# Four units with u kept as pairs of tokens and transposed as 32-bit words, with two decays on VectorE and two output copies on ScalarE

## The chip, the cores and the metric

The kernel runs on one core of a Trainium2 chip. The core has a matrix engine (TensorE, PE in the profile, with its weight loads as PEld), VectorE (DVE), ScalarE (ACT), GpSimd (POOL) and SyncE (SP), which here only issues DMAs. The metric is the device time of one execution in microseconds (us); of several runs the median is given.

## What is computed

A gated recurrence over tokens, followed by a highway layer. The inputs are x and f_logit (4 sequences of 6336 tokens, 256 channels, float32), a lower bound for each channel, two 256 x 256 weights and a bias.

```python
sig = 1.0 / (1.0 + np.exp(-f_logit))
f = lower_bound + (1.0 - lower_bound) * sig
i = 1.0 - f
for t in range(S):                       # each of the 4 sequences on its own
    h = f[:, t] * h + i[:, t] * x[:, t]
    y[:, t] = h
H = np.maximum(y @ w_h, 0.0)
T = 1.0 / (1.0 + np.exp(-(y @ w_t + b_t)))
out = T * H + (1.0 - T) * y
```

## The kernel before

The 25344 tokens are cut into 21 units. A unit has one sub-unit or, in the middle of the kernel (units 7 to 13), two; a full sub-unit is 1024 tokens. A sub-unit is loaded with tokens across the 128 partitions, eight tokens to a partition, so a tile of x or of f_logit is 128 x 8 x 256. The scan needs the other layout, channels across partitions and tokens along them, and the 256 channels make two halves. So TensorE transposes on the way in, and the product with an identity brings the result back on the way out.

All work is written out by hand in one string, `order`. Each token of it is one step, and each engine carries out its steps in that order. A token is a letter, the unit, and then sub-unit and half (or chunk and half); the number behind the colon is a buffer or, for steps that write PSUM, the banks; a `v` at the end puts a step on VectorE that stands elsewhere without it. The letters:

- `l`, `x`: loads of f_logit and x (SyncE issues them). `w`: the store of a block of output.
- `u` (L273, ScalarE): u = sigmoid(-f_logit), written as 16-bit floats. `f8.1` means unit 8, half 1; `u8.1` unit 8, sub-unit 1.
- `i` (L297, TensorE): transposes u into PSUM, one 128 x 128 block for each of eight tokens. `f` (L312 on ScalarE, L310 on VectorE): the decay, f = 1 - (1 - lower_bound) u, read from these banks and written to SBUF with the tokens in order. The transposed blocks lie token by token (j, then p), and f wants p, then j, so f reads with a hop at every element.
- `b`, `B` (L288, GpSimd): the product of u and x, half a sub-unit or a whole one. It is stored in pairs of tokens, so that `p` (L322, TensorE) can transpose two 16-bit tokens as one 32-bit word, four transposes for a half in place of eight.
- `s` (L331, VectorE): the scan along the tokens, over the decays and over the transposed products in PSUM, in pieces where a sequence begins inside a unit. It carries the state from unit to unit.
- `z`, `g` (L344 and L149, TensorE): the two products with the weights. `t` (L367, ScalarE): the sigmoid of z. `d` (L374, VectorE): the larger of g and a multiple of y. `e`, `E` (L388, GpSimd, or VectorE with `v`): d times t.
- `o` (L407 and L408, TensorE): back to tokens across partitions, summed in PSUM. `c` (L427 on ScalarE, L425 on VectorE): the copy of that to SBUF, from which the store goes.

PSUM has eight banks, and the string says which bank each step uses. A step that writes a bank waits until the step that read it before is done. Four such places matter later. In unit 8 the transposes i8.1.1 and i8.0.1 fill banks 6 and 7, f8.1 reads them, and g6.0.0 writes the same two. The outputs o4.0.0 and o4.0.1 share banks 2 and 3, with the copy c4.0.0 between them. The sigmoid t11.1.0 reads banks 6 and 7 before z12.1.0 writes them. The product g12.0.0 feeds d12.0.0 and needs the scan s12.1 before it.

The order of these steps around the first place stands in the string so:

```python
o4.0.0:23 p7.1.1:67 z6.0.1:45 x8.0:4 u8.1:2 c4.0.0v:2 t6.0.1:0 d6.0.1:2 p7.0.1 o4.0.1:23 c4.0.1:1 s7.1:2 i7.0.0:01
x8.1:0 i7.1.0 f7.0:2 p7.1.0:45 w3.0.1 w3.0.0 i8.0.0:23 i8.1.0 l9.0:1 p7.0.0 s7.0:3 l9.1:2 E5.0 f8.0:0 z6.0.0:01 t6.0.0
i8.1.1:67 i8.0.1 f8.1:1 o5.0.0:23 o5.0.1:01 B8.0:0 b8.1.1:1 g6.0.0:67 b8.1.0 d6.0.0 E6.0 g7.1.1:45 d7.1.1:3 w4.0.1
```

Of the kernel before, what the change touches and what calls it, by code (L numbers as in the profile page):

```python
# [91 lines left out]
w11.0.1 u17.0:3 z13.0.1:45 x20.0:3 d13.1.1:2 g13.0.1:23 d13.0.1 B15.0:0 w11.1.0 l20.0:0 w11.1.1 g13.1.0:01 t13.0.1:1
u16.0:1 o12.1.0:67 d13.1.0 p14.0.1:4 s14.1:4 c12.1.0:3 x16.0:0 z13.1.0:23 t13.1.0:2 o12.0.1:01 p14.0.0:5 z13.0.0:67
z13.1.1:23 c12.0.1:2 t13.0.0 s14.0:5 t13.1.1 o12.1.1:01 c12.1.1:1 i17.0.1:4 e13.0.1 o12.0.0:67 i17.0.0:2 p15.0.1:3
# [175 lines left out]
    def do_u(eng, slot, n, s):  # L270
        nb = units[n][1][s]
        u = sb([P, NB, D], FP16, "u", slot)
        pin(nc.scalar.activation(u[:, :nb], st[n]["l", s][:, :nb], AF.Sigmoid, scale=-1.0))  # L273
# [8 lines left out]
    def products(eng, slot, n, s, k0, k1):
        if ("bv", s) not in st[n]:
            st[n]["bv", s] = sb([P, NB // 2, D, 2], BF16, "bv", slot)
        cuts = {2: (0, 1), 4: (0, 1, 2), 8: (0, 2, 4)}[units[n][1][s]]
# [2 lines left out]
        shared(pin(e.tensor_mul(st[n]["bv", s][:, a:c].rearrange("p k d j -> p k j d"),  # L288
                                st[n]["u", s][:, 2 * a:2 * c].rearrange("p (k j) d -> p k j d", j=2),
                                st[n]["x", s][:, 2 * a:2 * c].rearrange("p (k j) d -> p k j d", j=2))), not eng)  # L290

    def do_i(eng, slot, n, s, h):
        if ("uT", h) not in st[n]:
            st[n]["uT", h] = Banks(slot, FP16)
        uT = st[n]["uT", h].one(s)
        for j in range(units[n][1][s]):
            pin(nc.tensor.transpose(uT[:, j * P:(j + 1) * P], st[n]["u", s][:, j, h * P:(h + 1) * P], ident_h))  # L297

    def do_f(eng, slot, n, h):
        N, subs = tokens(n), units[n][1]  # L300
        f = sb([P, 2 * NB * P], FP16, "f", slot)
        to, of = f[:, :N], st[n]["uT", h].all(N)
        if len(subs) == 1:
            to = to.rearrange("c (p j) -> c p j", j=subs[0])
            of = of.rearrange("c (j p) -> c p j", j=subs[0])
        else:
            to = to.rearrange("c (s p j) -> c s p j", s=len(subs), j=subs[0])
            of = of.rearrange("c (s j p) -> c s p j", s=len(subs), j=subs[0])
        if eng:
            pin(nc.vector.tensor_scalar(to, of, ncc[:, h:h + 1], 1.0, op0=ALU.mult, op1=ALU.add))  # L310
        else:
            pin(nc.scalar.activation(to, of, AF.Identity, scale=ncc[:, h:h + 1], bias=1.0))  # L312
        st[n]["f", h] = f

    def do_p(eng, slot, n, s, h):
        if ("bT", h) not in st[n]:
# [1 line left out]
        words = st[n]["bT", h].one(s).bitcast(FP32)
        g = units[n][1][s] // 2
        for k in range(g):  # L320
            pair = st[n]["bv", s][:, k, h * P:(h + 1) * P].rearrange("p d j -> p (d j)").bitcast(FP32)
            pin(nc.tensor.transpose(words[:, k:k + g * (P - 1) + 1:g], pair, ident_f))  # L322
# [152 lines left out]
```

## Time and profile before

| | us |
|---|---|
| median of 3 runs | 207.34 (206.93 to 207.41) |
| span of the profiled execution (first to last instruction) | 205.8 |
| busy: PE / DVE / ACT / POOL | 194.8 / 192.4 / 190.7 / 173.8 |
| scans (L331), 40 of one form group | 103.7 |
| products of u and x on GpSimd (L288), 39 | 101.4 |
| gates on GpSimd (L388), 33 | 71.5 |
| decays on ScalarE (L312), 38 | 50.3 |
| u on ScalarE (L273), 28 | 48.1 |
| output copies on ScalarE (L427), 46 | 44.2 |

Of the profiled execution the views give its span; what lies around the span shows in the difference to the runs. A row of a group names line, engine, operation, what is written and read with its shape, how often, the busy time, the mean time of one in ns, and the idle time before with what ended it. A row of a timeline has start, length, engine, line and operation; equal neighbours are merged with their count. TensorE's matmuls overlap, so a row's length there is longer than its share of the engine's time. The granted clock of TensorE is 0.998 over the span.

### The profile page before, as it was taken

The page shows a single profiled execution, that of the slowest core. Times are in us where ns is not written, and L with a number is a line of the kernel's source. Part 1 is how long each engine was busy: PE and PEld are TensorE (multiplying, and loading weights), DVE is VectorE, ACT ScalarE, POOL GpSimd, SP SyncE. Part 2 cuts the span into 40 slices and gives each one's busy share as a digit, 9 for nine tenths or more (in the row PEclk, how much of TensorE's full clock was granted, in tenths as well). Part 3 has the DMA queues.
Part 4 walks back from the last instruction along what each step waited for, and adds up shares of the span by engine and source line. Part 5 has one row for each costly group of instructions (what it writes and reads, how often), then busy time and mean ns, then how long its engine had stood idle before and what let it go on. Part 6 is the DMA issues. An engine that isn't in the chain of part 4 may idle for free.

```text
span 205.8 us, 4646 instructions
## 1 busy us (share of the span) xinstructions
PE 194.8 (95%) x1850; PEld 135.7 (66%) x1850; DVE 192.4 (93%) x147; ACT 190.7 (93%) x182; POOL 173.8 (84%) x85
## 2 busy tenths in 40 slices
PE   7989999969989999999999999999999999999992
PEld 2555775746765747757757858657757868777671
DVE  0679999999999999999999999999999999999992
ACT  5197999999999999999999999999999999999992
POOL 3634696999999999979999869999899788999760
PEclk9999999999999999999999999999999999999999
DMA  6999999999999999999999999999999999853766
GB/s 191 375 427 419 417 420 419 414 413 426 416 426 427 414 422 410 432 408 427 426 408 426 427 412 425 419 422 427 414 411 407 334 411 382 344 212 140 277 225 234
DMA packets 16700, 78.67 MB, mean 382 GB/s; under 512 B 1828, under 2 KB 2344, under 8 KB 10792
## 3 DMA queue, kind: packets, MB, share of 16 engines
q1 hardware_dynamic: 16672, 78.39, 93.9%
q8 instruction: 14, 0.23, 0.4%
q14 instruction: 6, 0.05, 0.1%
q10 hardware_dynamic: 8, 0.00, 0.0%
HBM read 52.43 MB, written 25.95 MB: 381 GB/s over the span
## 4 chain that ended last, share of the span: by engine, by line
PE 56%; DVE 24%; ACT 7%; issue 5%; DMA 5%; SPq 0%; DVEq 0%; ACTq 0%
PE psum L344 17%; DVE y L331 15%; PE psum L149 13%; DVE d L374 7%; PE psum L407 7%; PE psum L408 7%; PE psum L322 6%; PE psum L297 5%; ACT f L312 4%; DMA x<-in_x_dram 4%; ACT t L367 2%; DMA l<-in_f_logit_dram 1%; ACT u L273 1%; PE psum L250 1%; ACT o L427 1%
## 5 line engine op out<-in xcount | busy, mean ns | idle before, releaser
L288 POOL TENSOR_TENSOR bv<-u,x 128x1024 bf16<-128x1024 f16 (+2 forms) x39 | 101.4, 2615 | 20.0 <-DVE d L388 10.9
L331 DVE TENSOR_TENSOR_SCAN y<-f,y,psum 128x1024 bf16<-128x1024 f16 (+6 forms) x40 | 103.7, 2612 | 0.5 <-PE psum L407 0.4
L344 PE MATMUL psum<-y,w_sb 128*128 128x512 bf16 (+1 forms) x240 | 79.6, 368 | 4.2 <-ACT f L312 1.9
L388 POOL TENSOR_TENSOR d<-d,t 128x1024 bf16<-128x1024 bf16 (+3 forms) x33 | 71.5, 2180 | 4.6 <-ACT o L427 1.3
L374 DVE SCALAR_TENSOR_TENSOR d<-y,ncc,psum 128x1024 bf16<-128x1024 bf16 (+2 forms) x60 | 62.7, 1084 | 1.1 <-PE psum L344 0.4
L149 PE MATMUL psum<-y,w_sb 128*128 128x512 bf16 x168 | 63.6, 379 | 0.0
L367 ACT ACTIVATE t<-psum,bt 128x1024 bf16<-128x1024 f32 (+2 forms) x60 | 57.4, 988 | 0.9 <-PE psum L344 0.5
L273 ACT ACTIVATE u<-l 128x2048 f16<-128x2048 f32 (+2 forms) x28 | 48.1, 1744 | 6.5 <-DMA l<-in_f_logit_dram 6.5
L312 ACT ACTIVATE f<-psum,ncc 128x1024 f16<-128x1024 f16 (+3 forms) x38 | 50.3, 1344 | 1.2 <-PE psum L297 1.2
L407 PE MATMUL psum<-diag,y 128*128 128x128 f16 x396 | 49.7, 219 | 0.2
L408 PE MATMUL psum<-ident_b,d 128*128 128x128 bf16 x396 | 49.7, 219 | 0.0
L408 PEld LDWEIGHTS <-d 128*128 128x128 bf16 x396 | 43.5, 112 | 3.8 <-DVE d L388 0.4
L427 ACT COPY o<-psum 128x1024 f32<-128x1024 f32 (+1 forms) x46 | 44.2, 997 | 1.6 <-ACT f L312 0.6
L407 PEld LDWEIGHTS <-y 128*128 128x128 bf16 x396 | 43.6, 112 | 2.7
L344 PEld LDWEIGHTS <-w_sb 128*128 128x128 f16 x240 | 23.0, 98 | 20.1 <-issue 0.8
L322 PE MATMUL psum<-ident_f,bv 128*128 128x128 f32 x198 | 29.4, 275 | 0.8 <-ACT f L312 0.7
L149 PEld LDWEIGHTS <-w_sb 128*128 128x128 f16 x168 | 16.4, 97 | 20.2 <-issue 5.9
L297 PE MATMUL psum<-ident_h,u 128*128 128x128 f16 x396 | 28.8, 221 | 0.8 <-DVE y L331 0.4
L297 PEld LDWEIGHTS <-u 128*128 128x128 f16 x396 | 25.1, 99 | 5.7 <-issue 1.2
L322 PEld LDWEIGHTS psum<-ident_f,bv 128*128 128x128 f32 x198 | 22.4, 141 | 5.8 <-ACT f L312 1.4
L388 DVE TENSOR_TENSOR d<-d,t 128x1024 bf16<-128x1024 bf16 (+3 forms) x20 | 11.3, 596 | 0.1
L149 PE MATMUL psum<-zeros 128*128 128x512 bf16 x39 | 10.6, 398 | 0.0
(34 smaller groups left out, 43.1 us busy)
## 6 DMA issues: line engine op xcount, KB each, us to landing
l<-in_f_logit_dram SPq DMA_DIRECT2D x23, 1024.0 KB, 13.6
x<-in_x_dram SPq DMA_DIRECT2D x23, 1024.0 KB, 14.2
out_dram<-o SPq DMA_DIRECT2D x43, 512.0 KB, 8.0
out_dram<-x SPq DMA_DIRECT2D x7, 256.0 KB, 2.0
out_dram<-o SPq DMA_DIRECT2D x6, 256.0 KB, 9.3
l<-in_f_logit_dram SPq DMA_DIRECT2D x2, 512.0 KB, 6.5
x<-in_x_dram SPq DMA_DIRECT2D x2, 512.0 KB, 7.3
l<-in_f_logit_dram SPq DMA_DIRECT2D x3, 256.0 KB, 2.8
```

The lines of the kernel that those rows point to most:

```text
L149: return pe.add_instruction(mybir.InstMatmult(name=nc.get_next_instruction_name(), start_tensor_calc=start, stop_tensor_calc=stop, tile_si ...
L288: shared(pin(e.tensor_mul(st[n]["bv", s][:, a:c].rearrange("p k d j -> p k j d"), st[n]["u", s][:, 2 * a:2 * c].rearrange("p (k j) d -> p ...
L297: pin(nc.tensor.transpose(uT[:, j * P:(j + 1) * P], st[n]["u", s][:, j, h * P:(h + 1) * P], ident_h))
L312: pin(nc.scalar.activation(to, of, AF.Identity, scale=ncc[:, h:h + 1], bias=1.0))
L322: pin(nc.tensor.transpose(words[:, k:k + g * (P - 1) + 1:g], pair, ident_f))
L331: pin(nc.vector.tensor_tensor_scan(y[:, c:e], st[n]["f", h][:, c:e], data, 0.0 if fresh else carry[h], op0=ALU.mult, op1=ALU.add))
L344: pin(nc.tensor.matmul(p.part(a, e), w, data, start=ki == 0, stop=ki == NH - 1))
L367: pin(nc.scalar.activation(half(n, q, "t", m), z, AF.Sigmoid, bias=bt[:, m:m + 1]))
L374: pin(nc.vector.scalar_tensor_tensor(half(n, q, "d", m), y, ncc[:, m:m + 1], g, op0=ALU.mult, op1=ALU.max))
L388: shared(pin(e.tensor_mul(d, d, t)), not eng)
L407: pin(nc.tensor.matmul(o, st[n]["y", h][:, whole], diag[:, h], start=True, stop=False))
L408: pin(nc.tensor.matmul(o, half(n, q, "d", h)[:, cols], ident_b, start=False, stop=True))
```

## The change

In units 8, 10, 14 and 15 u is stored as pairs: for each pair of tokens and each channel the two tokens lie side by side. In units 8 and 14 ScalarE reads f_logit in its own order and writes every second element; in units 10 and 15 it writes in order and reads the two tokens of a pair in turn, 1 KB apart. In all four, TensorE transposes u as it does the products, two tokens in a 32-bit word, and the words land in PSUM so that the tokens are in order. The decay of such a unit then reads and writes in order. The product of u and x reads u and writes in order and reads x at two tokens in turn, 1 KB apart.

Four steps change engines: f8.1 and f14.0 go from ScalarE to VectorE, c4.0.0 and c9.1.1 from VectorE to ScalarE. The string is otherwise the same.

```diff
+    PAIRS_WRITTEN, PAIRS_READ = (8, 14), (10, 15)
+    PAIRS = PAIRS_WRITTEN + PAIRS_READ
...
-o4.0.0:23 p7.1.1:67 z6.0.1:45 x8.0:4 u8.1:2 c4.0.0v:2 t6.0.1:0 d6.0.1:2 p7.0.1 o4.0.1:23 c4.0.1:1 s7.1:2 i7.0.0:01
+o4.0.0:23 p7.1.1:67 z6.0.1:45 x8.0:4 u8.1:2 c4.0.0:2 t6.0.1:0 d6.0.1:2 p7.0.1 o4.0.1:23 c4.0.1:1 s7.1:2 i7.0.0:01
...
         u = sb([P, NB, D], FP16, "u", slot)
-        pin(nc.scalar.activation(u[:, :nb], st[n]["l", s][:, :nb], AF.Sigmoid, scale=-1.0))
+        to, of = u[:, :nb], st[n]["l", s][:, :nb]
+        if n in PAIRS:
+            u = u.rearrange("p j d -> p (j d)").rearrange("p (k d j) -> p k d j", d=D, j=2)
+            of = of.rearrange("p (k j) d -> p k j d", j=2)
+            to = u[:, :nb // 2]
+            if n in PAIRS_WRITTEN:
+                to = to.rearrange("p k d j -> p k j d")
+            else:
+                of = of.rearrange("p k j d -> p k d j")
+        pin(nc.scalar.activation(to, of, AF.Sigmoid, scale=-1.0))
...
+        if n in PAIRS:
+            shared(pin(e.tensor_mul(st[n]["bv", s][:, a:c], st[n]["u", s][:, a:c],
+                                    st[n]["x", s][:, 2 * a:2 * c].rearrange("p (k j) d -> p k d j", j=2))), not eng)
+            return
...
+    def paired(out, of, s, h, g):
+        words = out.one(s).bitcast(FP32)
+        for k in range(g):
+            pair = of[:, k, h * P:(h + 1) * P].rearrange("p d j -> p (d j)").bitcast(FP32)
+            pin(nc.tensor.transpose(words[:, k:k + g * (P - 1) + 1:g], pair, ident_f))
...
+        if n in PAIRS:
+            paired(st[n]["uT", h], st[n]["u", s], s, h, units[n][1][s] // 2)
+            return
...
         to, of = f[:, :N], st[n]["uT", h].all(N)
-        if len(subs) == 1:
+        if n in PAIRS:
+            pass
+        elif len(subs) == 1:
```

**At 50 to 65 us.** On VectorE, from the two steps d5.0.0 and d5.0.1 (first row) to the scans of unit 8. The COPY is c4.0.0, the four scans are s7.1 and s7.0, two pieces each, and the three d behind them are d6.0.0, d7.1.1 and d7.0.1. Before:

```order
35 L374 SCALAR_TENSOR_TENSOR d<-y,ncc,psum 128x1024 x2
36 L425 COPY o<-psum 128x1024
37 L374 SCALAR_TENSOR_TENSOR d<-y,ncc,psum 128x1024
38 L331 SCALAR_TENSOR_TENSOR y<-f,y,psum 128x1216
39 L331 SCALAR_TENSOR_TENSOR y<-f,psum 128x832
40 L331 SCALAR_TENSOR_TENSOR y<-f,y,psum 128x1216
41 L331 SCALAR_TENSOR_TENSOR y<-f,psum 128x832
42 L374 SCALAR_TENSOR_TENSOR d<-y,ncc,psum 128x1024 x3
43 L331 SCALAR_TENSOR_TENSOR y<-f,y,psum 128x2048 x2
```

The same stretch of VectorE with the change, where the first row takes in d6.0.1 as well and f<-psum is f8.1:

```order
35 L396 SCALAR_TENSOR_TENSOR d<-y,ncc,psum 128x1024 x3
36 L353 SCALAR_TENSOR_TENSOR y<-f,y,psum 128x1216
37 L353 SCALAR_TENSOR_TENSOR y<-f,psum 128x832
38 L353 SCALAR_TENSOR_TENSOR y<-f,y,psum 128x1216
39 L353 SCALAR_TENSOR_TENSOR y<-f,psum 128x832
40 L336 TENSOR_SCALAR f<-psum,ncc 128x2048
41 L396 SCALAR_TENSOR_TENSOR d<-y,ncc,psum 128x1024 x3
42 L353 SCALAR_TENSOR_TENSOR y<-f,y,psum 128x2048 x2
```

The copy has left the place ahead of d6.0.1, and f8.1 has come in between the scans of s7.0 and d6.0.0.

On TensorE, at the end of o5.0.1 and the beginning of g6.0.0, with the engines that a row waits for in brackets. Before:

```order
855 L408 MATMUL psum<-ident_b,d 128x128
856 L344 LDWEIGHTS w_sb
857 L344 MATMUL psum<-y,w_sb 128x512 [waits Activation_49]
858 L149 LDWEIGHTS w_sb
859 L149 MATMUL psum<-y,w_sb 128x512
```

And with the change:

```order
795 L430 MATMUL psum<-ident_b,d 128x128
796 L366 LDWEIGHTS w_sb
797 L366 MATMUL psum<-y,w_sb 128x512 [waits DVE_49]
798 L151 LDWEIGHTS w_sb
799 L151 MATMUL psum<-y,w_sb 128x512
```

The order on TensorE is the same, but the first matmul of g6.0.0 now waits for VectorE where it waited for ScalarE.

**At 131 to 138 us.** On ScalarE, from t11.0.0 and t11.1.1 (first row) to the copy c11.0.1; the first COPY is c9.1.0, the two u are u15.0 and u14.0, the t between them is t11.1.0. Before:

```order
82 L367 ACTIVATE t<-psum,bt 128x1024 x2
83 L427 COPY o<-psum 128x1024
84 L273 ACTIVATE u<-l 128x2048
85 L367 ACTIVATE t<-psum,bt 128x1024
86 L273 ACTIVATE u<-l 128x2048
87 L367 ACTIVATE t<-psum,bt 128x1024
88 L427 COPY o<-psum 128x1024
```

With the change:

```order
82 L389 ACTIVATE t<-psum,bt 128x1024 x2
83 L449 COPY o<-psum 128x1024 x2
84 L284 ACTIVATE u<-l 128x2048
85 L389 ACTIVATE t<-psum,bt 128x1024
86 L284 ACTIVATE u<-l 128x4x2x256
87 L389 ACTIVATE t<-psum,bt 128x1024
88 L449 COPY o<-psum 128x1024
```

The copy c9.1.1 has come in ahead of c9.1.0, so u15.0 and t11.1.0 stand one step later; u14.0 is now written in pairs.

More of the change, by code (lines that the diff above doesn't have):

```diff
@@ L64 @@
 f7.1:3 z5.0.1:45 t5.0.1:2 p6.0.0:1 z5.0.0:23 t5.0.0 s6.0:1 g5.0.0:67 d5.0.0:1 g5.0.1:45 d5.0.1 g6.0.1:01 B7.0:2 u8.0:0
-o4.0.0:23 p7.1.1:67 z6.0.1:45 x8.0:4 u8.1:2 c4.0.0v:2 t6.0.1:0 d6.0.1:2 p7.0.1 o4.0.1:23 c4.0.1:1 s7.1:2 i7.0.0:01
+o4.0.0:23 p7.1.1:67 z6.0.1:45 x8.0:4 u8.1:2 c4.0.0:2 t6.0.1:0 d6.0.1:2 p7.0.1 o4.0.1:23 c4.0.1:1 s7.1:2 i7.0.0:01
 x8.1:0 i7.1.0 f7.0:2 p7.1.0:45 w3.0.1 w3.0.0 i8.0.0:23 i8.1.0 l9.0:1 p7.0.0 s7.0:3 l9.1:2 E5.0 f8.0:0 z6.0.0:01 t6.0.0
-i8.1.1:67 i8.0.1 f8.1:1 o5.0.0:23 o5.0.1:01 B8.0:0 b8.1.1:1 g6.0.0:67 b8.1.0 d6.0.0 E6.0 g7.1.1:45 d7.1.1:3 w4.0.1
+i8.1.1:67 i8.0.1 f8.1v:1 o5.0.0:23 o5.0.1:01 B8.0:0 b8.1.1:1 g6.0.0:67 b8.1.0 d6.0.0 E6.0 g7.1.1:45 d7.1.1:3 w4.0.1
 x9.0:1 g7.0.1:67 d7.0.1:0 c5.0.0:0 c5.0.1:3 p8.0.1:23 u9.0:1 p8.1.1 u9.1:3 z7.1.1:45 t7.1.1:1 s8.1:4 z7.1.0:67 t7.1.0
@@ L86 @@
 w10.0.1 i13.1.1 s12.0:2 b13.1.1:1 f13.1:3 p12.0.1 z11.0.0:01 b13.1.0 t11.0.0 z11.1.1:67 t11.1.1:1 s12.1:3 l17.0:3
-o9.1.0:45 o9.1.1:01 c9.1.1v:3 w9.1.1 c9.1.0:1 w9.1.0 B13.0:0 E11.0 z11.1.0:67 l16.0:4 x15.0:2 u15.0:2 g12.0.0:23
+o9.1.0:45 o9.1.1:01 c9.1.1:3 w9.1.1 c9.1.0:1 w9.1.0 B13.0:0 E11.0 z11.1.0:67 l16.0:4 x15.0:2 u15.0:2 g12.0.0:23
 t11.1.0 e11.1.0 d12.0.0:1 u14.0:0 e11.1.1 g12.1.0:45 d12.1.0:3 g12.1.1:01 B14.0:2 p13.0.1:23 z12.1.0:67 t12.1.0:2
@@ L90 @@
 p13.1.0 o11.1.1:67 o11.0.0:45 x17.0:4 c11.1.1:0 s13.1:0 c11.0.0:3 i14.0.1:2 f14.1:0 i15.0.1:3 o11.1.0:67 c11.1.0:1
-f15.1:1 s13.0:1 g12.0.1:45 e12.1.1v e12.1.0 d12.0.1 i14.0.0:2 e12.0.1 f14.0:3 g13.0.0:01 d13.0.0:0 g13.1.1:67 w11.0.0
+f15.1:1 s13.0:1 g12.0.1:45 e12.1.1v e12.1.0 d12.0.1 i14.0.0:2 e12.0.1 f14.0v:3 g13.0.0:01 d13.0.0:0 g13.1.1:67 w11.0.0
 w11.0.1 u17.0:3 z13.0.1:45 x20.0:3 d13.1.1:2 g13.0.1:23 d13.0.1 B15.0:0 w11.1.0 l20.0:0 w11.1.1 g13.1.0:01 t13.0.1:1
@@ L317, in do_p @@
             st[n]["bT", h] = Banks(slot, BF16)
[L318 to L322, printed above, removed]
+        paired(st[n]["bT", h], st[n]["bv", s], s, h, units[n][1][s] // 2)
     carry = {}
```

## The prediction

> **What bounds the kernel now.** I read the page first, then the busy time by stretches, the timelines of the engines at the places that the change touches, and the groups by form. The span is 205.8 us; the median of the runs is 207.34 us, so 1.5 us lie around the span, and I add them at the end.
>
> ```profile
> PE 194.8 (95%) x1850; PEld 135.7 (66%) x1850; DVE 192.4 (93%) x147; ACT 190.7 (93%) x182; POOL 173.8 (84%) x85
> 70.00:80.00 10.00, 10.00 (x87) 6.50 (x85) 9.76 (x6) 10.00 (x9) 9.99 (x5) 1.00 1.01 418
> 130.00:140.00 10.00, 10.00 (x85) 6.45 (x84) 9.90 (x7) 10.00 (x8) 10.00 (x4) 1.00 1.02 422
> ```
>
> In the rows of the stretches the columns behind the length are PE, PEld, DVE, ACT, POOL (each with its count), the granted clock, the DMA share and GB/s. PE, DVE, ACT and POOL are all full at once: there is no single bound. What counts, then, is not an engine's sum but who waits for whom at the edited places: a bubble that is put into the order of VectorE or TensorE there has next to no idle time behind it (0.24 us of VectorE's in the first stretch, 0.10 in the second) into which it could vanish.
>
> **The pieces with a price of their own.** First the transposes.
>
> ```profile
> L322 PE MATMUL psum<-ident_f,bv 128*128 128x128 f32 x198 | 29.4, 275 | 0.8 <-ACT f L312 0.7
> L297 PE MATMUL psum<-ident_h,u 128*128 128x128 f16 x396 | 28.8, 221 | 0.8 <-DVE y L331 0.4
> ```
>
> A 32-bit transpose takes 29.4 / 198 = 0.148 us of PE's busy time, two 16-bit ones 2 x 28.8 / 396 = 0.146. Six sub-units times two halves give 48 32-bit transposes for 96 16-bit ones, at the same PE time: 0. That the paired writes of u (sub-units 8.0, 8.1 and 14.0) cost ScalarE more I also put at 0; they are bounded with the paired reads among the rivals.
>
> ```profile
> L310 DVE TENSOR_SCALAR f<-psum,ncc 128x1024 f16<-128x1024 f16 x1 | 1.3, 1271 | 0.0
> L388 DVE TENSOR_TENSOR d<-d,t 128x2048 bf16<-128x2048 bf16 x1 | 1.2, 1200 | 0.0
> L388 DVE TENSOR_TENSOR d<-d,t 128x1024 bf16<-128x1024 bf16 x11 | 7.6, 719 | 0.0
> ```
>
> A decay f on VectorE: the one there is (L310) hops through PSUM and takes 1.27 us for 1024 elements; 2048 would be at most twice that, 2.54. The paired f reads and writes 16-bit elements in unit steps, as the gates (L388) do: 1.20 for 2048, 0.72 for 1024. I take the gates' price, since unit steps are just what the layout changes, and keep the other end as a rival. [...]
>
> **Place one: f8.1 goes to VectorE, c4.0.0 to ScalarE (50 to 65 us).**
>
> ```profile
> 50.04 1.22 DVE L425 COPY o<-psum 128x1024 f32<-128x1024 f32 x1 [0.28 <-PE psum L408]
> 56.90 2.72 DVE L331 TENSOR_TENSOR_SCAN y<-f,y,psum 128x1216 bf16<-128x1216 f16 x1
> 59.53 1.86 DVE L331 TENSOR_TENSOR_SCAN y<-f,psum 128x832 bf16<-128x832 f16 x1
> 61.46 3.74 DVE L374 SCALAR_TENSOR_TENSOR d<-y,ncc,psum 128x1024 bf16<-128x1024 bf16 x3
> 65.13 4.47 DVE L331 TENSOR_TENSOR_SCAN y<-f,y,psum 128x2048 bf16<-128x2048 f16 x1
> 51.60 1.13 ACT L367 ACTIVATE t<-psum,bt 128x1024 bf16<-128x1024 f32 x1
> 53.59 3.83 ACT L312 ACTIVATE f<-psum,ncc 128x2048 f16<-128x2048 f16 x2
> 58.31 1.98 ACT L312 ACTIVATE f<-psum,ncc 128x2048 f16<-128x2048 f16 x1
> 51.53 0.22 PE L407 MATMUL psum<-diag,y 128*128 128x128 f16 x1
> 52.50 1.05 PE L297 MATMUL psum<-ident_h,u 128*128 128x128 f16 x16
> 60.33 0.38 PE L344 MATMUL psum<-y,w_sb 128*128 128x512 bf16 x1 [0.46 <-ACT f L312]
> 60.98 0.38 PE L149 MATMUL psum<-y,w_sb 128*128 128x512 bf16 x1
> ```
>
> Before: c4.0.0 is the copy at 50.04; the scans of s7.0 run from 56.90 to 61.39; beside them ScalarE makes f8.1 (58.31 to 60.29), PE starts g6.0.0 at 60.33 because f8.1 has then freed banks 6 and 7, is done with it at 60.98 + 0.38 = 61.36, and d6.0.0 starts at 61.46. VectorE waits for nothing.
>
> After: f8.1 stands on VectorE behind those scans and ahead of d6.0.0. Nothing else can be done in between, since VectorE keeps its order: f8.1 takes 1.20, then PE must begin g6.0.0 (0.04 to hand over, 60.29 to 60.33; 1.03 of work; 0.10 back, 61.36 to 61.46). So from the end of s7.0 to the start of d6.0.0 it is 1.20 + 1.17 = 2.37 us where it was 0.07: +2.30.
>
> What does the copy's leaving give back? 1.14 us on VectorE at 50 us, but s7.0 needs f7.0, and f7.0 gets later. On ScalarE c4.0.0 can begin where t6.0.1 began, at 51.60, and end at 52.61 (1.0 us, as its copies take). PE's o4.0.1 writes the same banks; it started at 51.53 and now starts at 52.65, so the transposes behind it (i7.0.0 and i7.1.0, at 52.50, done at 53.55) end 1.12 later. f7.0, the first of the two at 53.59, waited for just these: 54.71 + 1.98 = 56.69, and s7.0 can start at 56.75, 0.15 before its old 56.90. Place one is 2.30 - 0.15 = **+2.15 us** at d6.0.0. Behind it d7.1.1, g7.0.1 and d7.0.1 follow as before, so s8.1 moves from 65.13 to 67.3, and with it both VectorE, which is full from here to the end, and PE, whose work on unit 8 waits for these scans.
>
> **Place two: c9.1.1 goes to ScalarE, f14.0 to VectorE (133 to 150 us).**
>
> ```profile
> 134.36 1.19 DVE L425 COPY o<-psum 128x1024 f32<-128x1024 f32 x1
> 135.66 3.66 DVE L374 SCALAR_TENSOR_TENSOR d<-y,ncc,psum 128x1024 bf16<-128x1024 bf16 x3
> 139.24 3.54 DVE L331 TENSOR_TENSOR_SCAN y<-f,y,psum 128x1600 bf16<-128x1600 f16 x1
> 133.55 1.04 ACT L427 COPY o<-psum 128x1024 f32<-128x1024 f32 x1
> 134.44 1.96 ACT L273 ACTIVATE u<-l 128x2048 f16<-128x2048 f32 x1
> 136.25 1.15 ACT L367 ACTIVATE t<-psum,bt 128x1024 bf16<-128x1024 f32 x1
> 133.56 0.22 PE L408 MATMUL psum<-ident_b,d 128*128 128x128 bf16 x1
> 135.24 0.38 PE L149 MATMUL psum<-y,w_sb 128*128 128x512 bf16 x1
> 137.62 0.38 PE L344 MATMUL psum<-y,w_sb 128*128 128x512 bf16 x1
> 138.48 0.60 PE L322 MATMUL psum<-ident_f,bv 128*128 128x128 f32 x4
> ```
>
> On VectorE the copy at 134.36 fills a bubble: behind it d12.0.0 (135.66) needs g12.0.0, which PE ends at 135.24 + 0.38 = 135.62. Its leaving gives 0. On ScalarE c9.1.1 must wait for o9.1.1 (133.56 + 0.22 = 133.78), so it starts at 133.82 where c9.1.0 started at 133.55; with 0.89 for the copy itself (133.55 to 134.44) all that follows is 1.16 later. t11.1.0 then ends at 136.25 + 1.15 + 1.16 = 138.56; it frees the banks for z12.1.0, which started at 137.62 and now starts at 138.60: +0.98 on PE, which has no idle time here. The transposes p13.1.1 at 138.48 end at 140.06 in place of 139.08, and s13.1 starts at 140.16 in place of 139.24: **+0.9 us** on VectorE too. Then f14.0 adds its 0.72, less some overlap with its neighbours, **+0.6**, and ScalarE, which gets 1.0 us back there, was not the one waited for.
>
> The sum: 2.15 + 0.9 + 0.6 = 3.65 us; 205.8 + 3.65 + 1.5 = **211.0 us**. That the gaps that PE has elsewhere take up some of it gives a low end of this case of 208.6.
>
> **The rivals.**
>
> ```profile
> L288 POOL TENSOR_TENSOR bv<-u,x 128x2048 bf16<-128x2048 f16 x12 | 49.5, 4132 | 3.9 <-DVE d L388 3.9
> L388 POOL TENSOR_TENSOR d<-d,t 128x2048 bf16<-128x2048 bf16 x5 | 20.4, 4083 | 0.1
> 54.38 8.33 POOL L288 TENSOR_TENSOR bv<-u,x 128x2048 bf16<-128x2048 f16 x3
> 83.28 4.28 POOL L288 TENSOR_TENSOR bv<-u,x 128x1024 bf16<-128x1024 f16 x2
> 89.00 4.27 POOL L288 TENSOR_TENSOR bv<-u,x 128x1024 bf16<-128x1024 f16 x2 [1.44 <-DVE d L388]
> 93.67 0.61 PE L322 MATMUL psum<-ident_f,bv 128*128 128x128 f32 x4
> L273 ACT ACTIVATE u<-l 128x2048 f16<-128x2048 f32 x23 | 44.1, 1947 | 0.7 <-DMA l<-in_f_logit_dram 0.6
> 81.79 1.09 PE L322 MATMUL psum<-ident_f,bv 128*128 128x128 f32 x8 [0.40 <-ACT f L312]
> ```
>
> *GpSimd pays for the hop in x.* The paired products read x 1 KB further at every second element. Low end: their contiguous writes make them as cheap as the gates, 4.083 for 4.132, no gain to speak of. High end: x is one of two operands, and if its half of 4.13 us doubled, 2048 elements would cost 2.07 more. Unit 8's products (8.33 us) and unit 10's first two (4.28) would carry it to the two at 89.00, whose last is wanted by PE at 93.67. At half as much again: 87.55 + 0.5 x (8.33 + 4.28) = 93.9, then 1.5 x 4.27 = 6.4, so 100.3 where PE, by then 2.15 late, wants it at 95.8: +4.5, 215.5 us. At a quarter: +0.6, 211.6. I take 0, as the strided writes cost nothing in the first row against the second; chance 0.20 for a price of a quarter or more. [...]
>
> *ScalarE pays for strided u.* Nearest are the f at L312, which hop through PSUM at every element and take 1.98 us, as much as a u in unit steps (1.95): 0. The other end is a doubled u, +1.95. The reads of units 10 and 15 stand ahead of work that PE waits for (f10.0 at 81.79, t11.1.0 above), so three times half of that, 2.9 us, gives 213.9, all of it 216.8; the writes of unit 8 stand ahead of c4.0.0 and would come to less, since there are two. Chance 0.11.
>
> *f in unit steps is not faster on VectorE* (the change does not do what it is laid out for): +1.34 at f8.1 and 0.55 at f14.0, 212.9 us. Chance 0.07.
>
> *The other side: work decides, not order.* VectorE loses 1.22 + 1.19 and gets 1.20 + 0.72: -0.5 us; ScalarE loses about 3.1 and gets 2.1: -1.0. If the engines' sums set the end, that is 206.3 to 206.8 us. For it: the sums are within 2% of each other. It decides only from where s7.0 starts 2.3 us earlier, at 54.6, and f7.0's transposes, now behind o4.0.1, do not let it. Partly true, it gives no change. Chance 0.22: 0.09 faster, 0.13 no change.
>
> **How the numbers follow.** The forecast has the rest, 0.40, at 211.0. A measurement of this kernel can tell about 0.3%, 0.6 us, from no change; faster ends at 206.7, slower begins at 208.0. Slower: 0.40 + 0.20 + 0.11 + 0.07 = 0.78. The range 207.5 to 216.0 leaves out the faster cases, half of those with no change and the dearest prices of x and u, about 0.2 together.
>
> **What would show it.** Right: the timeline of VectorE has f 128x2048 followed by an idle 1.1 to 1.2 us that g6.0.0 (L366 of the new kernel) ends; the scan of 2048 behind it starts near 67.3; PE idles about 1 us ahead of z12.1.0, released by a t. Wrong: d6.0.0 starts within 1 us of 61.46, or the groups show the paired products over 4.6 us, a paired u over 2.2, or f 128x2048 near 2.5.

## The result and the profile after

The changed kernel takes **215.74 us** (median of 4 runs, 215.17 to 216.18), the kernel before beside it 207.38 (206.93 to 207.66): ratio 1.0404, 95% interval 1.0379 to 1.0429. It is 8.4 us slower; the forecast was 3.65 slower. The sign was right and the time lies in the range, but the change is 2.3 times as large as forecast.

The first row of the page: ScalarE has 2.8 us more work than before, GpSimd 1.6 and VectorE 1.0. PE's sum can't be compared, since matmul records are missing (1774 for 1802 weight loads, where it is 1850 for 1850 before). All of them are busy for a smaller share of a span of 213.4 us (205.8 before), so most of the added time is in waits.

```profile
PE 193.1 (91%) x1774; PEld 135.0 (63%) x1802; DVE 193.4 (91%) x147; ACT 193.5 (91%) x182; POOL 175.4 (82%) x85
```

The groups by form of the changed kernel (busy time, then the mean ns of one). The line numbers are those of the new file: L284 is u, L303 the unpaired and L300 the paired product, L311 the 32-bit transposes, L336 f on VectorE.

```profile
L284 ACT ACTIVATE u<-l 128x2048 f16<-128x2048 f32 x23 | 47.1, 2079 | 0.9 <-DMA l<-in_f_logit_dram 0.9
L303 POOL TENSOR_TENSOR bv<-u,x 128x2048 bf16<-128x2048 f16 x9 | 37.2, 4134 | 3.9 <-DMA x<-in_x_dram 3.9
L300 POOL TENSOR_TENSOR bv<-u,x 128x2048 bf16<-128x2048 f16 x3 | 13.2, 4403 | 0.0
L311 PE MATMUL psum<-ident_f,u 128*128 128x128 f32 x48 | 6.7, 275 | 1.1 <-ACT u L284 0.7 <-DVE y L353 0.5
L336 DVE TENSOR_SCALAR f<-psum,ncc 128x2048 f16<-128x2048 f16 x1 | 1.3, 1260 | 0.0
```

The 23 u of 2048 elements took 44.1 us before and take 47.1: the six paired ones cost 0.5 each. A paired product costs 4.40 for 4.13, 0.27 more. The 48 transposes of u take 6.7 / 48 = 0.14 us each, as forecast, and f8.1 takes 1.26.

Place one, the timelines of VectorE, ScalarE and TensorE (start, length, engine, line; in brackets the idle time before, and what ended it):

```profile
46.94 3.63 DVE L396 SCALAR_TENSOR_TENSOR d<-y,ncc,psum 128x1024 bf16<-128x1024 bf16 x3
54.28 2.75 DVE L353 TENSOR_TENSOR_SCAN y<-f,y,psum 128x1216 bf16<-128x1216 f16 x1 [3.70 <-PE psum L429]
58.72 2.72 DVE L353 TENSOR_TENSOR_SCAN y<-f,y,psum 128x1216 bf16<-128x1216 f16 x1
63.13 1.26 DVE L336 TENSOR_SCALAR f<-psum,ncc 128x2048 f16<-128x2048 f16 x1
65.51 3.75 DVE L396 SCALAR_TENSOR_TENSOR d<-y,ncc,psum 128x1024 bf16<-128x1024 bf16 x3 [1.12 <-PE psum L151]
69.17 4.47 DVE L353 TENSOR_TENSOR_SCAN y<-f,y,psum 128x2048 bf16<-128x2048 f16 x1
```

```profile
47.52 4.93 ACT L284 ACTIVATE u<-l 128x2048 f16<-128x2048 f32 x2
52.29 1.01 ACT L449 COPY o<-psum 128x1024 f32<-128x1024 f32 x1
55.35 3.83 ACT L338 ACTIVATE f<-psum,ncc 128x2048 f16<-128x2048 f16 x2
```

```profile
53.35 0.22 PE L429 MATMUL psum<-diag,y 128*128 128x128 f16 x1 [2.13 <-ACT o L449]
64.45 0.38 PE L366 MATMUL psum<-y,w_sb 128*128 128x512 bf16 x1 [2.71 <-DVE f L336]
```

The bubble around f8.1 is there as forecast: 1.26 of f8.1 and 1.12 of idle that g6.0.0 ends. But ahead of it stands a wait of 3.70 us that the forecast doesn't have. s7.1 (54.28) needs o4.0.1 (L429) on TensorE: it writes y buffer 2 (`s4.0:2` and `s7.1:2` in the string), which o4.0.1 still reads. o4.0.1 writes the banks of c4.0.0 and waits 2.13 us for it; and c4.0.0, now on ScalarE, stands behind u8.0 and u8.1, which take 4.93 us where they took 3.73. So s7.0 starts at 58.72 in place of 56.90, and d6.0.0 at 65.51 in place of 61.46. Before, s7.1 and the two u stood so, with no wait ahead of s7.1:

```profile
52.45 2.75 DVE L331 TENSOR_TENSOR_SCAN y<-f,y,psum 128x1216 bf16<-128x1216 f16 x1
47.99 3.73 ACT L273 ACTIVATE u<-l 128x2048 f16<-128x2048 f32 x2
```

Place two, VectorE, ScalarE and TensorE:

```profile
140.59 3.82 DVE L396 SCALAR_TENSOR_TENSOR d<-y,ncc,psum 128x1024 bf16<-128x1024 bf16 x3 [1.22 <-PE psum L151]
145.55 3.55 DVE L353 TENSOR_TENSOR_SCAN y<-f,y,psum 128x1600 bf16<-128x1600 f16 x1 [1.14 <-PE psum L311]
150.58 3.55 DVE L353 TENSOR_TENSOR_SCAN y<-f,y,psum 128x1600 bf16<-128x1600 f16 x1 [0.50 <-PE psum L311]
156.79 0.74 DVE L336 TENSOR_SCALAR f<-psum,ncc 128x1024 f16<-128x1024 f16 x1
```

```profile
138.80 1.93 ACT L449 COPY o<-psum 128x1024 f32<-128x1024 f32 x2 [0.18 <-ACT t L389]
140.61 2.39 ACT L284 ACTIVATE u<-l 128x2048 f16<-128x2048 f32 x1
142.89 1.11 ACT L389 ACTIVATE t<-psum,bt 128x1024 bf16<-128x1024 f32 x1
143.89 2.56 ACT L284 ACTIVATE u<-l 128x2048 f16<-128x2048 f32 x1
```

```profile
144.05 0.81 PE L366 MATMUL psum<-y,w_sb 128*128 128x512 bf16 x2 [0.95 <-ACT t L389]
```

The two copies in one place (138.80), u15.0 at 2.39 and u14.0 at 2.56 (1.96 and 1.95 before) delay the t between and behind them, and the scans s13.1 (145.55) and s13.0 (150.58) wait 1.14 and 0.50 us for transposes that stand behind products into the banks of these t. The first of these products is z12.1.0, ahead of which TensorE idles 0.95 us until t11.1.0 is done, as forecast. f14.0 takes 0.74.

### The profile page after: what moved, and what is told of

Its sections match the earlier page's. It is cut to its first block, busy times and chain, and to the rows that moved or that the text cites. A ratio compares the mean times of both kernels' runs of the same rounds, so it can differ in the third digit from the quotient of the medians.

```text
span 213.4 us, 4521 instructions
## 1 busy us (share of the span) xinstructions
PE 193.1 (91%) x1774; PEld 135.0 (63%) x1802; DVE 193.4 (91%) x147; ACT 193.5 (91%) x182; POOL 175.4 (82%) x85
## 4 chain that ended last, share of the span: by engine, by line
PE 41%; DVE 21%; ACT 14%; issue 10%; DMA 10%; SPq 1%; ACTq 0%; DVEq 0%
PE psum L366 13%; DVE y L353 13%; DMA l<-in_f_logit_dram 8%; PE psum L151 8%; DVE d L396 7%; PE psum L429 7%; PE psum L430 6%; ACT u L284 6%; PE psum L311 6%; ACT f L338 4%; ACT t L389 3%; PE psum L321 2%; DMA x<-in_x_dram 2%; SPq L263 1%; ACT o L449 1%
## 5 line engine op out<-in xcount | busy, mean ns | idle before, releaser
L303 POOL TENSOR_TENSOR bv<-u,x 128x1024 bf16<-128x1024 f16 (+2 forms) x30 | 76.3, 2557 | 17.9 <-DMA x<-in_x_dram 7.6
L366 PE MATMUL psum<-y,w_sb 128*128 128x512 bf16 (+1 forms) x235 | 78.2, 368 | 8.7 <-DVE f L336 2.7
L284 ACT ACTIVATE u<-l 128x2048 f16<-128x2048 f32 (+2 forms) x28 | 51.1, 1852 | 6.1 <-DMA l<-in_f_logit_dram 6.1
L151 PE MATMUL psum<-y,w_sb 128*128 128x512 bf16 x147 | 55.7, 379 | 0.1
L429 PE MATMUL psum<-diag,y 128*128 128x128 f16 x396 | 49.8, 219 | 2.9 <-ACT o L449 2.1
L449 ACT COPY o<-psum 128x1024 f32<-128x1024 f32 (+1 forms) x48 | 46.0, 987 | 2.5 <-ACT t L389 1.1
L338 ACT ACTIVATE f<-psum,ncc 128x1024 f16<-128x1024 f16 (+3 forms) x36 | 47.0, 1324 | 0.9 <-PE psum L321 0.9
L429 PEld LDWEIGHTS <-y 128*128 128x128 bf16 x396 | 43.6, 111 | 2.7
L311 PE MATMUL psum<-ident_f,bv 128*128 128x128 f32 x198 | 29.5, 275 | 1.7 <-POOL bv L303 0.8
L300 POOL TENSOR_TENSOR bv<-u,x 128x1024 bf16<-128x1024 f16 (+1 forms) x9 | 26.8, 2999 | 1.3 <-DVE d L410 1.3
L311 PEld LDWEIGHTS psum<-ident_f,bv 128*128 128x128 f32 x198 | 22.2, 141 | 7.0 <-ACT f L338 1.4
L321 PE MATMUL psum<-ident_h,u 128*128 128x128 f16 x300 | 22.0, 219 | 0.8 <-ACT u L284 0.6
L321 PEld LDWEIGHTS <-u 128*128 128x128 f16 x300 | 19.0, 98 | 4.7 <-ACT u L284 1.1
```

Source lines behind the costliest of these rows:

```text
L151: return pe.add_instruction(mybir.InstMatmult(name=nc.get_next_instruction_name(), start_tensor_calc=start, stop_tensor_calc=stop, tile_si ...
L284: pin(nc.scalar.activation(to, of, AF.Sigmoid, scale=-1.0))
L366: pin(nc.tensor.matmul(p.part(a, e), w, data, start=ki == 0, stop=ki == NH - 1))
L429: pin(nc.tensor.matmul(o, st[n]["y", h][:, whole], diag[:, h], start=True, stop=False))
```

## The experiments

Theory A: the new chain (u8.0, u8.1, c4.0.0, o4.0.1, s7.1) and the bubble of f8.1 make place one; the dearer u adds wherever it stands ahead of a step that is waited for. Rival B: the layout itself, through the sums of ScalarE and GpSimd. Times are medians; "before" is the kernel before, run beside each group of experiments at 207.26 to 207.50.

**The layout without the moves, and the moves without the layout.** From the changed kernel, in the first the four steps get their old engines back, in the second no unit is paired:

```diff
-c4.0.0:2    f8.1v:1   c9.1.1:3    f14.0v:3
+c4.0.0v:2   f8.1:1    c9.1.1v:3   f14.0:3
...
-PAIRS_WRITTEN, PAIRS_READ = (8, 14), (10, 15)
+PAIRS_WRITTEN, PAIRS_READ = (), ()
```

> The pairs of units 8, 10, 14 and 15 as in the change, all four moved steps back on their old engines. Theory A (the moved steps cost through a chain: the copy c4.0.0 on ScalarE stands behind u8.0 and u8.1, o4.0.1 waits for it, the scan s7.1 waits for o4.0.1 because it writes the y that o4.0.1 reads, and f8.1 then keeps TensorE and VectorE waiting for each other; the dearer u adds only where it stands ahead of a step that is waited for): the two u of unit 8 delay f8.1 on ScalarE by about 1.1 us, those of unit 10 cost 0.9, u15.0 and u14.0 0.5 to 1.0, so about 2.5 to 3.0 us over the kernel before, 210 to 210.4. Theory B (the layout costs, wherever the steps stand, through ScalarE's sum and GpSimd's products): most of the 8.4 us, 213 or more. The forecast on record (u costs nothing): 207.4.

> The four steps moved as in the change, u unpaired everywhere, so f8.1 and f14.0 hop through PSUM on VectorE. Theory A: c4.0.0 starts 1.2 us earlier than in the changed kernel because u8.0 and u8.1 have their old price, so s7.1 starts near 53.1 us behind an idle of about 2.5 us ended by o4.0.1; f8.1 takes up to 2.5 us in place of 1.26, f14.0 1.27 in place of 0.74; the first d behind f8.1 is about 4 us late, place two adds 1.1 + 1.2: about 213.5 us (212.5 to 214.5). Theory B: 208 to 209.5. The forecast's own terms with an unpaired f: 212.9 with s7.1 at 51.3.

Measured: the layout alone 210.08, ratio 1.0133 (1.0106 to 1.0159); the moves alone 215.03, 1.0353 (1.0316 to 1.0391). VectorE with the layout alone, then with the moves alone:

```profile
56.41 2.72 DVE L353 TENSOR_TENSOR_SCAN y<-f,y,psum 128x1216 bf16<-128x1216 f16 x1
62.10 3.74 DVE L396 SCALAR_TENSOR_TENSOR d<-y,ncc,psum 128x1024 bf16<-128x1024 bf16 x3 [1.19 <-PE psum L151]
```

```profile
53.27 2.75 DVE L353 TENSOR_TENSOR_SCAN y<-f,y,psum 128x1216 bf16<-128x1216 f16 x1 [2.57 <-PE psum L429]
57.71 2.73 DVE L353 TENSOR_TENSOR_SCAN y<-f,y,psum 128x1216 bf16<-128x1216 f16 x1
62.12 2.33 DVE L336 TENSOR_SCALAR f<-psum,ncc 128x2048 f16<-128x2048 f16 x1
```

With the layout alone s7.0 is not late (56.41), but f8.1, on ScalarE behind the dearer u, is, and d6.0.0 waits 1.19 us for g6.0.0 behind it (62.10, where it started at 61.46 before). B falls: the layout is worth 2.6 us, not 8.4. With the moves alone s7.1 waits 2.57 us for o4.0.1, although u has its old price: the wait through the y buffer comes from the move of the copy, and the dearer u lengthens it. Together the two cost more than the change (2.6 + 7.5 for 8.4). The paired layout makes f8.1 1.07 us cheaper (2.33 to 1.26) and f14.0 0.53, which would account for it; but the moves alone also have more falls of the clock (five of six runs at 0.982 to 0.989, against two of four at 0.984 for the changed kernel), and these runs don't part the two. The moves alone are slower than expected by 0.5 us over the upper end; the section on the hardware says why.

**The chain at place one, link by link.** Four kernels, each the changed one with one edit: a y buffer of its own for s7.1; c4.0.0 back on VectorE; c4.0.0 between u8.0 and u8.1; f8.1 back on ScalarE.

```diff
-s7.1:2
+s7.1:6
...
-c4.0.0:2
+c4.0.0v:2
...
-u8.1:2 c4.0.0:2
+c4.0.0:2 u8.1:2
...
-f8.1v:1
+f8.1:1
```

> The changed kernel, with a y buffer of its own (a seventh) for the scan s7.1, so that it need not wait for o4.0.1. Theory A: s7.1 starts right behind d6.0.1, near 51.3 us in place of 54.28; s7.0 is then limited by f7.0 (done at 57.2), so it starts at 57.3 in place of 58.7, and the whole kernel is about 1.4 us faster: 214.3. Rival (the buffer isn't what s7.1 waits for, or the wait is off the path): 215.7, s7.1 stays at 54.3.

> The changed kernel with c4.0.0 back on VectorE; f8.1 stays there too. Theory A: s7.1 starts near 52, s7.0 near 56.5 behind f7.0, f8.1 near 61, the first d behind it near 63.3 in place of 65.5: 2.2 us less, 213.5. If only the bubble around f8.1 counts (as the forecast had it, 0.15 us for the copy): 215.6 to 215.9.

> The changed kernel with the copy c4.0.0 one step earlier on ScalarE, between u8.0 and u8.1. Theory A (o4.0.1 and through it s7.1 wait for this copy): the copy ends near 50.9 us in place of 53.2, s7.1 starts near 52.2 in place of 54.28 and s7.0, then limited by f7.0 as with a y buffer of its own, near 57.3 in place of 58.7: 1 to 1.4 us less, 214.2 to 214.7. TensorE then idles about 0.3 us ahead of o4.0.1 in place of 2.13. Rival (ScalarE's sum of work decides, its order does not): 215.7.

> The changed kernel with f8.1 back on ScalarE; c4.0.0 stays there too. Theory A: s7.1 still waits until 54.3 and s7.0 still ends at 63.1, but f8.1 runs beside it on ScalarE (about 60.2 to 62.2), g6.0.0 ends near 63.3 and d6.0.0 starts near 63.4 in place of 65.5: 2.1 us less, 213.6. If the wait of s7.1 were the whole cost of place one: 215.7.

Measured: 214.58 with the buffer (1.0351, 1.0309 to 1.0394), 212.85 with the copy back (1.0270, 1.0236 to 1.0304), 213.99 with the copy earlier (1.0321, 1.0286 to 1.0356), 214.86 with f8.1 back (1.0354, 1.0314 to 1.0393). VectorE in these four kernels, in this order:

```profile
51.80 2.75 DVE L353 TENSOR_TENSOR_SCAN y<-f,y,psum 128x1216 bf16<-128x1216 f16 x1 [0.72 <-PE psum L311]
59.34 2.75 DVE L353 TENSOR_TENSOR_SCAN y<-f,y,psum 128x1216 bf16<-128x1216 f16 x1 [3.02 <-PE psum L311]
```

```profile
52.00 2.75 DVE L353 TENSOR_TENSOR_SCAN y<-f,y,psum 128x1216 bf16<-128x1216 f16 x1
60.86 1.26 DVE L336 TENSOR_SCALAR f<-psum,ncc 128x2048 f16<-128x2048 f16 x1
63.23 3.75 DVE L396 SCALAR_TENSOR_TENSOR d<-y,ncc,psum 128x1024 bf16<-128x1024 bf16 x3 [1.12 <-PE psum L151]
```

```profile
51.64 2.75 DVE L353 TENSOR_TENSOR_SCAN y<-f,y,psum 128x1216 bf16<-128x1216 f16 x1 [1.49 <-PE psum L429]
56.83 2.75 DVE L353 TENSOR_TENSOR_SCAN y<-f,y,psum 128x1216 bf16<-128x1216 f16 x1 [0.66 <-ACT f L338]
```

```profile
54.29 2.75 DVE L353 TENSOR_TENSOR_SCAN y<-f,y,psum 128x1216 bf16<-128x1216 f16 x1 [3.44 <-PE psum L429]
63.24 3.75 DVE L396 SCALAR_TENSOR_TENSOR d<-y,ncc,psum 128x1024 bf16<-128x1024 bf16 x3
```

With its own buffer s7.1 starts at 51.80 and waits for a transpose (L311, p7.0.1) and no longer for o4.0.1: the y buffer is the link. What s7.0 gains can't be read from this profile, since the granted clock fell to 0.50 there (from 55.00 to 58.00 us; s7.0 at 59.34); in time the kernel came out 1.2 us faster, with intervals that overlap. Its four executions at a granted clock of 1.0 took 213.63 to 214.59, against 215.17 and 215.32 of the changed kernel: 0.8 us by their medians. With the copy back on VectorE all three starts are as expected, and the kernel is 2.9 us faster where the forecast's term gave 0.15. With the copy earlier on ScalarE, the same work in another order, s7.0 starts at 56.83, limited by f7.0, and the kernel is 1.75 us faster: order decides, not ScalarE's sum. With f8.1 back d6.0.0 starts at 63.24, 2.27 earlier, which confirms the bubble; but the median fell by 0.9 only, and that one I had wrong by 1.3 us. The execution profiled, at a clock of 1.0, took 213.76, near the 213.6 expected; three of the six, at 0.985 to 0.987, took 215.5 to 215.9 (see the clock below).

**Place two and unit 10.** The changed kernel with c9.1.1 and f14.0 on their old engines, and with unit 10 unpaired:

```diff
-c9.1.1:3
+c9.1.1v:3
...
-f14.0v:3
+f14.0:3
...
-PAIRS_WRITTEN, PAIRS_READ = (8, 14), (10, 15)
+PAIRS_WRITTEN, PAIRS_READ = (8, 14), (15,)
```

> The changed kernel with c9.1.1 back on VectorE and f14.0 back on ScalarE. The forecast on record gives these two moves 0.9 + 0.6 = 1.5 us, and theory A keeps that: 214.2 (213.9 to 214.5); what the dearer u15.0 and u14.0 cost there, 0.8 to 1.1 us, stays. Theory B (the layout alone is to blame there): 215.7.

> The changed kernel with u of unit 10 unpaired again (units 8, 14 and 15 stay paired). Theory A: its two u are 0.47 us cheaper each, and t7.0.0 and t8.0.0 behind them are waited for: 0.9 us less, 214.9. If ScalarE's slack takes up the price of these two: 215.7.

Measured: 214.11 (1.0331, 1.0303 to 1.0359) and 215.25 (1.0366, 1.0339 to 1.0392). The moves of place two are worth 1.6 us, as the forecast had them (1.5). With them undone s13.1 no longer waits (first row). By VectorE's timelines, counted from s12.0, it starts 1.2 us earlier, and the scans of unit 14 1.9.

Unit 10 is worth 0.5 by the medians, with overlapping intervals: not told from nothing by the times alone. Its one execution with a granted clock of 1.0 took 214.1, against 215.17 and 215.32 of the changed kernel, which fits 0.9, but it is one execution. The timelines tell it. In the changed kernel (second and third row) TensorE idles 0.67 us for a paired u of unit 10, and the second scan of unit 9 then waits 0.48 for transposes. With unit 10 unpaired (last row) the two scans stand without a wait.

```profile
144.69 3.55 DVE L353 TENSOR_TENSOR_SCAN y<-f,y,psum 128x1600 bf16<-128x1600 f16 x1
83.89 0.66 PE L311 MATMUL psum<-ident_f,u 128*128 128x128 f32 x4 [0.67 <-ACT u L284]
87.95 4.48 DVE L353 TENSOR_TENSOR_SCAN y<-f,y,psum 128x2048 bf16<-128x2048 f16 x1 [0.48 <-PE psum L311]
84.11 8.84 DVE L353 TENSOR_TENSOR_SCAN y<-f,y,psum 128x2048 bf16<-128x2048 f16 x2
```

From the first scan of unit 9 to s12.0 it is 47.54 us in the changed kernel (83.00 to 130.54), 46.66 with unit 10 unpaired and 46.64 before: these u cost 0.9.

**The parts alone.** The kernel before with place one only (unit 8 paired, f8.1 and c4.0.0 moved), and with place two only (units 14 and 15 paired, f14.0 and c9.1.1 moved), each as an edit of the changed kernel:

```diff
-PAIRS_WRITTEN, PAIRS_READ = (8, 14), (10, 15)
+PAIRS_WRITTEN, PAIRS_READ = (8,), ()
-c9.1.1:3    f14.0v:3
+c9.1.1v:3   f14.0:3
...
-PAIRS_WRITTEN, PAIRS_READ = (8, 14), (10, 15)
+PAIRS_WRITTEN, PAIRS_READ = (14,), (15,)
-c4.0.0:2    f8.1v:1
+c4.0.0v:2   f8.1:1
```

> The kernel before with unit 8 paired, f8.1 on VectorE and c4.0.0 on ScalarE; nothing else of the change. Theory A: the step d6.0.0 is as late as in the changed kernel, 4.05 us by the two timelines, and nothing behind it takes that up: 207.4 + 4.05 = 211.4, up to 0.9 more where the clock falls (forecast on record: 209.5).

> The kernel before with units 14 and 15 paired, c9.1.1 on ScalarE and f14.0 on VectorE; nothing else of the change. Theory A: what the changed kernel loses on VectorE between s12.1 and d13.0.0, 2.6 us: 1.5 for the moves as forecast and 1.1 for u15.0 and u14.0: 210.0 (forecast on record: 208.9).

Measured: 212.49 (1.0246, 1.0214 to 1.0278) and 210.01 (1.0127, 1.0093 to 1.0161). VectorE with place one alone has the changed kernel's rows again:

```profile
54.35 2.75 DVE L353 TENSOR_TENSOR_SCAN y<-f,y,psum 128x1216 bf16<-128x1216 f16 x1 [3.90 <-PE psum L429]
65.58 3.75 DVE L396 SCALAR_TENSOR_TENSOR d<-y,ncc,psum 128x1024 bf16<-128x1024 bf16 x3 [1.11 <-PE psum L151]
```

5.0 and 2.5 us over the kernel before make 7.5 of the 8.4. The 0.9 left is what unit 10 costs by the timelines above; it was not run alone.

**One unit paired and no step moved.** Unit 17, whose f17.1 stands on VectorE in both kernels:

```diff
+PAIRS_WRITTEN, PAIRS_READ = (), (17,)
```

> The kernel before with one unit paired, 17, whose f17.1 stands on VectorE anyway; no step moves. f17.1 should take 0.74 us in place of 1.27 (as f14.0 in the changed kernel), u17.0 0.45 more on ScalarE. If VectorE is what is waited for there: 0.5 us less, 206.9, better than both kernels. If ScalarE is: 207.8. If both take it up: 207.4.

Measured: 207.66 over 12 runs, ratio 1.0008 (0.9988 to 1.0029): no change. f17.1 takes 0.74 in place of 1.27, but in the execution profiled VectorE then idles 0.39 and 0.32 us, behind f17.1 and behind the scan after it, where it had no idle time before: the time saved there isn't used. Whether the dearer u17.0 (2.41 for 1.95) makes these waits wasn't tested. None of the kernels beats the one before.

**TensorE kept busy in the two gaps.**

```diff
-p7.0.1 o4.0.1:23
+p7.0.1 k*8:0 o4.0.1:23
...
-o5.0.1:01 B8.0:0
+o5.0.1:01 c5.0.0:0 c5.0.1:3 k*10:2 B8.0:0
```

`k` is a product of zeros into the bank named; the two copies keep their place on ScalarE.

> The changed kernel with TensorE kept busy in the two gaps that the change opened: 8 products of zeros ahead of o4.0.1 and 10 ahead of g6.0.0, into banks that are free there. All waits stay as they were. Theory (the granted clock falls to half for some 3.4 us where one of the two gaps, 2.1 and 2.1 to 2.7 us, is noticed, in some executions and not in others): every execution shows a clock of 1.0 and the time of the undisturbed ones, 215.2 to 215.3, so 0.4 below the median of 215.74 and with a spread under 0.5. Rival (the falls have another cause): still two groups, near 215.2 and 216.2.

Measured: 215.35 (1.0385, 1.0358 to 1.0412), six runs from 214.92 to 215.66 with clocks of 0.995 to 1.0, as the kernel before has them. The second group near 216.2 is gone; the spread of 0.74 is wider than expected, and the interval overlaps that of the changed kernel.

## Why the prediction was wrong in size

- **The transposes (0): right.** 0.14 us each.
- **f in unit steps at the gates' price (1.20 and 0.72): right**, 1.26 and 0.74. On ScalarE they gained nothing here: with the layout alone f8.1 took 2.00 us there, where it had taken 1.98 hopping.
- **The bubble at f8.1 (+2.30): right.** f8.1 and the idle behind it make 1.26 + 1.12 = 2.38 us, where 0.07 lay before; putting f8.1 back takes 2.27 away.
- **"What does the copy's leaving give back?" (-0.15): this step failed.** The forecast put c4.0.0 on ScalarE at 51.60, followed it through o4.0.1's banks to the transposes and f7.0, and let s7.0 start at 56.75. It followed one path out of o4.0.1, the order of TensorE, and not the other: s7.1 writes the y buffer that o4.0.1 reads. s7.1 then waits for the copy as well, and s7.0 behind it starts at 58.72, 1.82 late in place of 0.15 early. With the moves alone, u at its old price, s7.0 starts 0.81 late (57.71): that part is the overlooked wait. The other 1.0 (57.71 to 58.72) is u8.0 and u8.1, 1.20 dearer together, in front of the copy.
- **The writes of u at 0, and the reads at 0: mis-sized, and the larger part of the miss.** A rival had up to 1.95 each; it is about 0.5. That rival had three reads on the path and the writes of unit 8 coming to less. The runs show both on it: at place one d6.0.0 waits 1.19 us even with all steps on their old engines, and the layout alone costs 2.6 us. The text named a paired u over 2.2 us as what would make it wrong, and these are 2.39 to 2.59.
- **Place two (+0.9 and +0.6): right for the moves** (1.6 by undoing them; by the timelines 1.2 at s13.1 and 0.7 more behind f14.0), and by the mechanism forecast, z12.1.0 behind t11.1.0; u15.0 and u14.0 come on top, so place two alone costs 2.5.
- **GpSimd's hop (chance 0.20): didn't happen.** 6.5% per product, 0.27 us, below the quarter from which that rival counted. No run shows a product at half as much again, from which that rival had 215.5 us: the paired ones of 2048 took 4.40 us in the changed kernel against 4.13 of the unpaired, and 4.38 to 4.45 in the others.
- **The other side, sums decide: refuted** by the copy that moves one step on the same engine for 1.75 us.

The sum by the timelines of the executions profiled: VectorE falls back by 4.05 us at place one, of which 2.15 was forecast; by 0.9 at the paired u of unit 10; and by 2.6 at place two, 1.9 from the moves and 0.8 from u15.0 and u14.0. That is the 7.6 us between the spans. The rest of the 8.4 lies outside of these two timelines: the changed kernel's median is 0.57 above its execution profiled, which had no fall of the clock, and 0.27 more lie around its span (215.17 - 213.39 against 207.34 - 205.83).

Of the 4.7 us missed, the price of u makes 2.7 (1.0 at place one through the copy's wait, 0.9 at unit 10, 0.8 at place two), the overlooked wait at u's old price 1.0 (0.81 late in place of 0.15 early), the moves of place two 0.4, and the last two terms 0.8; these are differences of single executions, and add up to within 0.2. That the time lies in the range is in part luck: its upper end was set by rivals with dearer x and u, and not by a wait through a y buffer.

## What to carry to other kernels

When a step moves to another engine, follow every release that hangs on it, buffers in SBUF as well as banks in PSUM: who next writes what the delayed reader still reads is as much a path as the reader's own queue (a wait of 3.70 us at s7.1 here). And a small price on an engine whose sum has room is not hidden if it stands in front of a step that others wait for (0.5 us for each of six u, 2.6 us in the time with the layout alone); where four engines are full, the place of a step in its engine's order counts beside the sums (1.75 us here for one place).

## What the runs showed of the hardware

**Behind gaps of 1.82 to 3.82 us on TensorE its granted clock fell to 0.50 for 3.41 us, in some executions.** The changed kernel's runs were 215.17 and 215.32 us at a granted clock of 1.0, and 216.15 and 216.18 at 0.984, as much as two such falls would take (2 x 3.41 / 2 of 214.4 us). The kernel with unit 10 unpaired shows it twice in its profile, the kernel with place one alone once, although its two gaps are equally long. TensorE's two gaps in the latter, and then five stretches of 3.41 us (length, PE, PEld, DVE, ACT, POOL, granted clock, DMA share, GB/s):

```profile
53.32 0.22 PE L429 MATMUL psum<-diag,y 128*128 128x128 f16 x1 [2.13 <-ACT o L449]
64.52 0.38 PE L366 MATMUL psum<-y,w_sb 128*128 128x512 bf16 x1 [2.13 <-DVE f L336]
```

```profile
50.54:53.95 3.41, 1.28 (x17) 1.07 (x16) 0.00 (x0) 3.41 (x3) 3.41 (x1) 1.00 1.00 406
53.95:57.36 3.41, 3.41 (x30) 3.41 (x28) 3.00 (x2) 2.32 (x3) 3.41 (x2) 0.50 1.03 432
57.36:60.78 3.42, 3.42 (x33) 2.88 (x32) 3.42 (x2) 3.42 (x3) 3.42 (x3) 1.00 1.00 417
60.78:64.19 3.41, 1.61 (x27) 1.43 (x25) 3.41 (x3) 3.23 (x4) 2.18 (x1) 1.00 1.02 423
64.19:67.60 3.41, 2.57 (x12) 1.09 (x12) 2.29 (x3) 2.86 (x2) 0.59 (x1) 1.00 1.02 425
```

The boundaries are those at which the clock recorded in this trace changed, carried on in equal steps. In all 14 profiles the clock between the first and the last change goes in whole steps of 3.41 us: each of the seven falls lasts one step, and the stretches at 1.0 beside them 2, 14, 17 or more. The first gap above (51.19 to 53.32) lies whole in one step, which leaves TensorE busy for 1.28 of its 3.41 us, and the next step runs at half the clock. The second, as long, is cut by a boundary at 64.19, which leaves 1.61 and 2.57 us busy, and no fall follows. Over all profiles the seven falls follow steps with 0.68 (the moves alone) to 1.59 us busy (the copy earlier); no fall follows a step with 1.61 or more, nor the one with 1.58 in the kernel with the copy back. In the profile of the changed kernel, which has no fall there, boundaries cut both gaps, and the least busy steps have 1.65 and 1.67. So in these traces the limit lies near 1.6 us busy, and they don't tell it more closely. The boundaries lie elsewhere in each execution (the first fall at 53.95 us here, at 54.54 with unit 10 unpaired), which would account for falls in some executions only.

With the gaps filled with products of zeros none of six runs shows a clock below 0.995, where one fall alone makes 0.992. The falls also explain, as far as single executions show it, why the kernels with gaps came out later than expected: the moves alone have a gap of 3.8 us, and five of their six runs show 0.982 to 0.989 and 214.3 to 216.0 us, the one at 1.0 takes 213.47, within what was expected.

**ScalarE paid for steps in SBUF**: u of 2048 took 2.56 us with 16-bit writes at every second element (u14.0) and 2.39 with 32-bit reads that alternate 1 KB apart (u15.0), against 1.95 in unit steps. It did not pay for the hop of f through PSUM: 1.98 us for 2048 before, where all hop, and 1.98 in the mean of the changed kernel, where some don't. **VectorE paid for that hop**: f8.1 took 2.33 us hopping (the moves alone) and 1.26 in unit steps.
